# A list scheduler's durations, hops and holding times set to traced values, with new priorities for the prologue

## The chip, the cores and the metric

The kernel runs on one core of one Trainium2 chip. The metric is device time in microseconds (us) of one launch; the time before is the median of three runs. A core has five engines that run their own instruction streams and wait for each other by semaphores: PE (matmul; its weight loads are listed as PEld), DVE (vector), ACT (scalar), POOL (GpSimd) and SP, which here issues all DMAs.

## What is computed

Three stages follow each other. Linear attention over 4 batches, 8 heads, 576 positions and 64 columns gives x of 2304 x 512. A mixture of 8 experts with weights from a softmax and 8 rounds of row and column normalisation (Sinkhorn) follows, and then a gated feed-forward layer.

```python
def _attn_ref(q, k, v):
    q_s = exp(q - max(q, -1)); q_s = q_s / (sum(q_s, -1) + 1e-09)
    k_s = exp(k - max(k, 2));  k_s = k_s / (sum(k_s, 2) + 1e-09)
    kv = einsum('bhsd,bhse->bhde', k_s, v)
    return einsum('bhsd,bhde->bhse', q_s, kv)

def _moe_ref(x, w_gate, w1, w2):
    P = exp(x @ w_gate - max)
    for _ in range(8):
        P /= P.sum(1, keepdims=True) + 1e-09
        P /= P.sum(0, keepdims=True) + 1e-09
        P *= N / E
    return sum(P[:, e:e+1] * (maximum(x @ w1[e], 0) @ w2[e]) for e in range(E))

def _moe2_ref(x, w_in, w_out):
    h = x @ w_in
    return (h * clip(h + 3, 0, 6) / 6) @ w_out
```

## The kernel before

**Matmuls.** Operands are split into a high and a low float16 half, so a product takes three matmuls for each 128 rows of depth. On top of that, 2 x 2 block products are formed in Strassen's way with seven products: `forms` makes the seven combinations of x (QB11, QT1, QB21, QB22, QT2, QT3, QT4) and `w1_steps` those of a weight block. Both end in `split`: ACT writes the high half, DVE the low half. One product is six matmuls of 384 columns.

**Steps.** The work behind the attention is 20 weight steps s (16 for the experts, 4 for the last layer) by 3 pairs p of token groups. `up_burst` makes the hidden layer of one (s, p), its copies out of PSUM run on ACT (`ring_r<-b`), and `down_tile` multiplies it with the second weights and adds to `acc`. While one (s, p) runs on PE, the weights of step s + 1 are loaded, scaled and split.

**The prologue.** Attention is done for two pairs of batches; the first stands ahead of everything. Its steps, with the tiles that they write: `load_k`, `load_q`, `load_v` (SP); `kmax` (DVE, `scr`), `ktr` (PE transposes), `mT` (DVE reduce, `ring_c`), `kback` (PE), `ksub` (DVE, `xbuf<-xbuf,b`), `kexp` (ACT, `xbuf<-xbuf`); `vcopy` (two chunks on ACT, two on POOL, `xbuf<-acc`); `kv` (PE, 64x65 matmuls, one set for each of four chunks c), which needs `kexp(c)` and `vcopy(c)`; `kvout` and `kvmax` (DVE), which divide and take the largest entry, one PE matmul with `identb` to spread it, and `pow2`, which makes a power-of-two scale `sx`. For the queries: `qmax` (DVE, `ring_qm<-acc`), `qsub` (POOL, `acc`), `qexp` (ACT, `acc<-acc`), `qsum` (DVE), `qn_` (DVE and POOL, `ring_r<-acc,ring_qm`), `qtr` (PE transposes `units,ring_r` and an ACT copy `ring_h<-b`). `xset` multiplies the transposed queries with the scaled kv (`ring_h,xbuf`, 64x192) and opens `forms`. Beside this the first weight block goes through `a1scale` (four squares on ACT, `w1buf<-raw`, then the same matmul with `identb`), `a1sums` (POOL) and `a1` (splits); the second weights through `a2`. The marks with 0 and 1 ahead are the attention of the first and the second pair; `w11` and `w21` are the two weight blocks of the second weight step.

**What sets the order.** Nothing is issued as it is written. `Planner` records every instruction, gives each a duration (`cost`, line 177) and a latest start worked out backwards from its users (`order`, line 295), less an entry of the table `EARLIER` (line 41) for the step's mark: a larger number puts a step ahead. `lay` (line 317) then places instructions one by one, with the engines' free times, a lock that DVE and POOL share, and waits between engines from `hop` (line 286). The order of placement is the order of issue on each engine. Where the plan has a pause of over 400 ns on PE ahead of 130 us, `issue` (line 444) puts matmuls in whose result nobody reads (`warm`, line 2383, in the trace `b<-units,plus`, L2385); their number is worked out from the planned pause. All other instructions carry line 472, where the recorded calls are issued, so they are told apart by their tiles.

Of the kernel before, what the change touches and what calls it, by code (L numbers as in the profile page):

```python
# [40 lines left out]
EARLIER = {  # L41
    "0kback": -30000.0,
    "0kexp": -52000.0,
    "0kmax": -26500.0,
    "0ksub": 500.0,
    "0kv_": 1000.0,
    "0kvout": -1000.0,
    "0load_k": 7000.0,
    "0load_q": -500.0,
    "0qsub": 19000.0,  # L50
    "0qsum": -9500.0,
    "0vcopy": -4000.0,
    "1load_v": 2000.0,
    "1qmax": -500.0,
    "1qn_": -15000.0,
    "1qsum": -11000.0,
    "a1load": 3000.0,
    "a1scale": -3500.0,
    "a1sums": -73500.0,
    "conv": 0000.0,  # L60
    "max": 40000.0,
    "w11": 500.0,
}
# [10 lines left out]
class Planner:  # L74
# [6 lines left out]
    SLACK = 60000.0  # L81
    HOP = 120.0
    MARGIN = 300.0
    NEAR = 4000.0
    GIVE = 100.0
# [91 lines left out]
    def cost(self, eng, name, out, ins):  # L177
        n = 1
# [3 lines left out]
        if eng == "tensor":  # L182
            passes = 1.0
            if out.dtype == F32 and ins[0].dtype == F32:
                passes = 2.0 if name == "transpose" else 4.0 if ins[0].shape[0] > 64 else 1.5
            return 2.0 + n * 0.4167 * passes
        if eng == "scalar":
            return 170 + 0.8 * n if psum else (720 if n == 512 else 180 + 0.9 * n)
        big = max([n] + [self.width(x) for x in ins])
# [96 lines left out]
    def hop(self, a, b):  # L286
        if a["eng"] == b["eng"] and a["eng"] != "sync":
            return 0.0
        if a["eng"] == "tensor":
            return 170.0 + self.HOP  # L290
        if a["eng"] == "sync":
            return a.get("land", 2500.0 + a["dma"] / 150.0)
        return self.HOP + (self.MARGIN if b["eng"] == "tensor" else 0.0)

# [22 lines left out]
    def lay(self, ops, first):  # L317
# [7 lines left out]
        ahead = {e: [] for e in self.ENGINES}  # L325
        lag = shift = pipe = 0.0
        gone = set()
        for o in ops:
# [13 lines left out]
        def following(q, t, d):  # L342
# [5 lines left out]
            for o in reversed(q[-24:]):  # L348
# [8 lines left out]
                if u == v:  # L357
                    break
                u += o["dur"]
                v += o["dur"]  # L360
                k += 1
# [4 lines left out]
        def pick(e):  # L366
            f = free[e]
            c = []
            for o in waits[e]:
# [3 lines left out]
                if first and o["fill"] and e != "sync" and o["late"] + lag > s + self.NEAR:  # L373
                    room, fits = following(e, s, o["dur"])
                    if not fits:
                        s = max(s + 50.0, room + 1.0)
                    elif o["lock"]:
                        room, fits = following(other[e] + " lock", s, o["dur"])
                        if not fits:
                            s = max(s + 50.0, room + 1.0)  # L380
# [5 lines left out]
            if e not in ("tensor", "sync"):  # L386
                end = s + o["dur"]
                for x in sorted((x for x in c if x[0] < end and x[1] < d), key=lambda x: x[1]):
# [4 lines left out]
        while len(result) < len(ops):  # L393
# [18 lines left out]
            o["start"] = s  # L412
            end = s + o["dur"] * (1.0 if e == "tensor" else 1.05)
            if e == "sync":
                free[e] = s + 500.0
                pipe = max(pipe, s + 2000.0) + o["dma"] / 370.0
                o["land"] = pipe + 1500.0 - s
                end = s
            else:
                free[e] = end  # L420
            if o["lock"]:
                lock[e] = end
            if e in other:
# [1995 lines left out]
```

## Time and profile before

| | |
|---|---|
| runs | 1769.96, 1770.32, 1772.51 us, median 1770.32 us |
| span of the profiled execution (its own time by the profiler) | 1768.3 us |
| PE busy | 1750.0 us (99%) |
| DVE, ACT, POOL busy | 1411.4 (80%), 1251.0 (71%), 588.0 (33%) us |
| chain that ended last | PE 96%, DVE 2%, DMA 1% |

The profiled execution is one run under the profiler, and its span runs from the first to the last instruction. The median of the timed runs lies 2.0 us above that span. A PE that is busy 99% of the span can still be filled with matmuls that nobody needs; the chain lists them by their line.

### The profile page before, as it was taken

The numbers are of one execution on the slowest core, as the hardware profiler recorded it, in microseconds if no ns is written. First come the engines' busy times: TensorE is split into PE (matmuls) and PEld (weight loads), VectorE is DVE, ScalarE is ACT, GpSimd is POOL, SyncE is SP. The second block draws the span as 40 slices with busy tenths as digits, with TensorE's granted clock in tenths as the row PEclk, the third lists the DMA queues.
The fourth block names the chain that finished last, engine by engine and source line by source line (L and its number), as shares of the span: only waits on it lengthen the run. The fifth ranks groups of instructions, "written<-read, shape, count | busy, mean of one in ns | idle before, by whom it ended". The sixth has DMA issues, their size and how long they took to land.

```text
span 1768.3 us, 33908 instructions
## 1 busy us (share of the span) xinstructions
PE 1750.0 (99%) x13199; PEld 1218.1 (69%) x13199; DVE 1411.4 (80%) x2629; ACT 1251.0 (71%) x2807; POOL 588.0 (33%) x651
## 2 busy tenths in 40 slices
PE   7999999999999999999999999999999999999999
PEld 5555556777777777777777777777777555777776
DVE  7874877787888888888888888888888788777884
ACT  5856575667667686777778687768777677767673
POOL 3423343434444423232333322333323223223311
PEclk9999999999999999999999999999999999999999
DMA  9410322324242313020303122130312454402022
GB/s 293 121 69 1 117 84 74 99 98 154 98 161 96 111 37 105 25 87 25 119 21 119 37 93 63 49 105 25 105 49 93 87 100 136 150 25 87 1 87 84
DMA packets 103330, 154.25 MB, mean 87 GB/s; under 512 B 47744, under 2 KB 51840, under 8 KB 102912
## 3 DMA queue, kind: packets, MB, share of 16 engines
q1 hardware_dynamic: 103168, 152.08, 27.8%
q8 instruction: 103, 1.69, 0.4%
q14 instruction: 59, 0.48, 0.1%
HBM read 119.69 MB, written 24.12 MB: 81 GB/s over the span
## 4 chain that ended last, share of the span: by engine, by line
PE 96%; DVE 2%; issue 1%; DMA 1%; ACT 0%; POOL 0%; SPq 0%; DVEq 0%; POOLq 0%; ACTq 0%
PE b L472 95%; PE b L2385 1%; DMA xbuf<-in_k_dram 0%; DVE prob L472 0%; DVE acc L472 0%; DVE ring_r L472 0%; DVE xbuf L472 0%; DMA acc<-in_q_dram 0%; DVE ring_rs L472 0%; SPq L472 0%; ACT w2buf L472 0%; DVE scr L472 0%; DVE ring_cs L472 0%; POOL wtmp L472 0%; DVE ring_c L472 0%
## 5 line engine op out<-in xcount | busy, mean ns | idle before, releaser
L472 PE MATMUL b<-xbuf,w1buf 128*128 128x384 f16 x5040 | 910.6, 326 | 0.4 <-DVE ring_r L472 0.2
L472 PEld LDWEIGHTS <-w1buf 128*128 128x128 f16 x5040 | 491.5, 98 | 278.2 <-issue 1.8
L472 PE MATMUL b<-w2buf,ring_h 128*128 128x256 f16 (+2 forms) x3048 | 523.5, 308 | 0.0
L472 POOL TENSOR_TENSOR ring_h<-ring_r,ring_h 128x384 f16<-128x384 f32 x262 | 259.8, 993 | 693.4 <-ACT ring_h L472 632.7
L472 PEld LDWEIGHTS <-ring_h 128*128 128x128 f16 x3810 | 371.4, 98 | 155.9 <-issue 1.8
L472 ACT COPY b<-b 128x256 f32<-128x256 f32 (+1 forms) x686 | 253.8, 376 | 191.5 <-PE b L472 114.6
L472 DVE SCALAR_TENSOR_TENSOR acc<-b,ring_cf,acc 128x512 f32<-128x512 f32 x372 | 270.9, 746 | 120.7 <-PE b L472 94.3
L472 PEld LDWEIGHTS <-xbuf 128*128 128x128 f16 x3228 | 303.2, 98 | 75.5 <-DVE xbuf L472 1.1
L472 ACT ACTIVATE ring_r<-b 128x384 f32<-128x384 f32 x319 | 155.2, 488 | 94.9 <-PE b L472 87.7
L472 DVE SCALAR_TENSOR_TENSOR ring_r<-b,ring_r 128x384 f32<-128x384 f32 x215 | 118.7, 553 | 65.3 <-PE b L472 37.6
L472 PE MATMUL b<-xbuf 128*128 128x256 f16 (+1 forms) x1338 | 118.8, 251 | 2.2 <-issue 1.6
L472 POOL TENSOR_TENSOR raw<-raw 128x256 f32<-128x256 f32 (+1 forms) x119 | 102.0, 874 | 52.7 <-DVE w2buf L472 18.9
L472 POOL TENSOR_TENSOR ring_h<-scr,ring_h 128x384 f16<-128x384 f32 x40 | 38.8, 970 | 225.2 <-ACT ring_h L472 216.6
L472 ACT ACTIVATE ring_h<-ring_r 128x384 f16<-128x384 f32 x210 | 108.2, 521 | 7.7 <-DVE ring_r L472 5.4
L472 PE MATMUL b<-scr,xbuf 128*128 128x256 f16 x762 | 107.2, 273 | 0.1
L472 PE MATMUL b<-w2buf,xbuf 128*128 128x256 f16 x762 | 107.2, 273 | 0.0
L472 PE MATMUL b<-kvs,xbuf 128*128 128x256 f16 x762 | 107.2, 273 | 0.0
L472 PE MATMUL b<-xbuf,ring_h 128*128 128x256 f16 x468 | 91.2, 273 | 0.0
L472 DVE SCALAR_TENSOR_TENSOR acc<-b,ring_co,acc 128x512 f32<-128x512 f32 (+1 forms) x82 | 60.3, 741 | 27.5 <-PE b L472 25.7
L472 DVE TENSOR_TENSOR xbuf<-scr,xbuf 128x384 f16<-128x384 f32 x126 | 76.9, 635 | 6.5 <-ACT xbuf L472 6.3
L472 DVE SCALAR_TENSOR_TENSOR w1buf<-raw,ring_ws,w1buf 128x512 f16<-128x512 f32 x100 | 79.2, 825 | 3.1 <-ACT w1buf L472 2.7
L472 ACT ACTIVATE scr<-b 128x384 f32<-128x384 f32 x113 | 54.8, 488 | 37.2 <-PE b L472 36.6
(197 smaller groups left out, 2128.2 us busy)
## 6 DMA issues: line engine op xcount, KB each, us to landing
xbuf<-xkeep SPq DMA_DIRECT2D x119, 384.0 KB, 3.5
raw<-in_moe_w_dram SPq DMA_DIRECT2D x31, 1024.0 KB, 5.5
scr<-in_moe_w_in_dram SPq DMA_DIRECT2D x13, 512.0 KB, 3.7
scr<-in_moe_w_out_dram SPq DMA_DIRECT2D x12, 512.0 KB, 3.4
xkeep<-xbuf SPq DMA_DIRECT2D x2, 2688.0 KB, 9.0
xkeep<-xbuf SPq DMA_DIRECT2D x14, 384.0 KB, 8.4
out_dram<-acc SPq DMA_DIRECT2D x18, 256.0 KB, 2.0
raw<-win SPq DMA_DIRECT2D x4, 1024.0 KB, 5.4
```

The lines of the kernel that those rows point to most:

```text
L472: f(*a, **k)
L2385: real.tensor.matmul(banks[t][:, : 2 * P], plus, some, start=True, stop=True, skip_group_check=True)
```

## The change

Three things are changed, and no instruction of the computation is added or removed.

1. `cost`, `hop` and the rules of `lay` get other numbers: durations for narrow float32 matmuls, ACT and POOL; a hop for each receiving engine (45 to 120 ns where 120 stood for all); a holding time `held`, which is less than the duration by 80 ns on DVE and ACT and 40 ns on POOL, since the next instruction may start that much ahead, and times 1.01 where durations were taken times 1.05; and for DMAs a limit of 8 in flight and another bandwidth.
2. The table `EARLIER` gets 35 entries in place of 21, nearly all of them for steps of the prologue.
3. As a result, instructions stand in another order on every engine, over the whole program, and the number of filling matmuls goes from 131 to 92.

```diff
 EARLIER = {
-    "0kback": -30000.0,
-    "0kexp": -52000.0,
...
-    "w11": 500.0,
+    "w11": -18000.0,
+    "w21": 21000.0,
 }
...
-    HOP = 120.0
+    HOP = {"vector": 45.0, "scalar": 45.0, "gpsimd": 95.0, "tensor": 65.0, "sync": 120.0}
+    OVERLAP = {"vector": 80.0, "scalar": 80.0, "gpsimd": 40.0}
+    IN_FLIGHT = 8
     MARGIN = 300.0
+    SLOW = 1.01
...
-                passes = 2.0 if name == "transpose" else 4.0 if ins[0].shape[0] > 64 else 1.5
+                passes = 2.0 if name == "transpose" else 4.0 if ins[0].shape[0] > 64 else 0.78
+            elif ins[0].shape[0] <= 64:
+                passes = 0.3
...
-            return 170 + 0.8 * n if psum else (720 if n == 512 else 180 + 0.9 * n)
+            return (170 + 0.8 * n if psum else 180 + 0.88 * n) + 90 * (len(ins) - 1)
...
-            if big == 512 and len(out.shape) > 2:
-                return 1610
-            return 70 + (2.25 if len(ins) > 1 else 1.2) * big
+            return 320 + 1.6 * big if len(ins) > 1 else 220 + 0.88 * big
...
+    def held(self, o):
+        return max(o["dur"] - self.OVERLAP.get(o["eng"], 0.0), 40.0) * (1.0 if o["eng"] == "tensor" else self.SLOW)
...
-            end = s + o["dur"] * (1.0 if e == "tensor" else 1.05)
+            end = s + o["dur"]
             if e == "sync":
+                if len(landed) >= self.IN_FLIGHT:
+                    s = max(s, landed[-self.IN_FLIGHT])
                 free[e] = s + 500.0
-                pipe = max(pipe, s + 2000.0) + o["dma"] / 370.0
-                o["land"] = pipe + 1500.0 - s
+                pipe = max(pipe, s + 1900.0) + o["dma"] / (310.0 if s < 4500.0 else 385.0)
+                landed.append(pipe + 200.0)
+                o["land"] = landed[-1] - s
                 end = s
             else:
-                free[e] = end
+                free[e] = s + self.held(o)
```

**Place 1: DVE behind the last `kmax`.** In the order of before DVE takes two query maxima (`ring_qm<-acc`), then the three remaining `mT` (`ring_c`), and the third of the remaining `ksub` (`xbuf<-xbuf,b`) stands behind a `qsum`:

```order
L472 TENSOR_TENSOR scr<-scr,xbuf 128x256
L472 TENSOR_REDUCE ring_qm<-acc 128x8x3 x2
L472 TENSOR_REDUCE ring_c_103<-b_67 128x2
L472 TENSOR_REDUCE ring_c_103<-b_68 128x2 x2
L472 TENSOR_TENSOR xbuf<-xbuf,b_65 128x1152
L472 TENSOR_TENSOR xbuf<-xbuf,b_66 128x1152
L472 TENSOR_REDUCE ring_qm<-acc 128x8x3
L472 TENSOR_TENSOR xbuf<-xbuf,b_66 128x1152
```

The same place on DVE in the changed order:

```order
L496 TENSOR_TENSOR scr<-scr,xbuf 128x256
L496 TENSOR_REDUCE ring_c_103<-b_67 128x2
L496 TENSOR_REDUCE ring_c_103<-b_68 128x2 x2
L496 TENSOR_REDUCE ring_qm<-acc 128x8x3 x2
L496 TENSOR_TENSOR xbuf<-xbuf,b_66 128x1152
L496 TENSOR_TENSOR xbuf<-xbuf,b_65 128x1152
L496 TENSOR_TENSOR xbuf<-xbuf,b_66 128x1152
L496 TENSOR_REDUCE ring_qm<-acc 128x8x3
```

The three `mT` have moved ahead of the two query maxima, and the three `ksub` follow each other.

**Place 2: ACT between the first `kexp` and the query copies.** In the order of before, three of the four weight squares (`w1buf_79,ring_c_107`), a `vcopy` (`xbuf<-acc`), a `qexp` (`acc<-acc`) and the fourth square stand ahead of the second `kexp`, and the last two `kexp` come last:

```order
L472 ACTIVATE w1buf_79,ring_c_107<-raw 128x512 x3
L472 COPY xbuf<-acc 128x18x64
L472 ACTIVATE acc<-acc 128x8x192
L472 ACTIVATE w1buf_79,ring_c_107<-raw 128x512
L472 ACTIVATE xbuf<-xbuf 128x1152
L472 ACTIVATE acc<-acc 128x8x192
L472 COPY xbuf<-acc 128x18x64
L472 ACTIVATE xbuf<-xbuf 128x1152 x2
L472 COPY ring_h<-b_68 128x384
```

The same place on ACT in the changed order, up to the fourth square:

```order
L496 ACTIVATE w1buf_79,ring_c_107<-raw 128x512 x2
L496 COPY xbuf<-acc 128x18x64
L496 ACTIVATE acc<-acc 128x8x192
L496 ACTIVATE xbuf<-xbuf 128x1152
L496 ACTIVATE acc<-acc 128x8x192
L496 ACTIVATE xbuf<-xbuf 128x1152 x2
L496 COPY xbuf<-acc 128x18x64
L496 ACTIVATE w1buf_79,ring_c_107<-raw 128x512
L496 COPY ring_h<-b_67 128x384
L496 COPY ring_h<-b_68 128x384
L496 ACTIVATE w1buf_79,ring_c_107<-raw 128x512
```

Two squares and the second `vcopy` have moved behind the last `kexp`, and the fourth square stands among the query copies (`ring_h<-b`).

**Place 3: ACT in the first (s, p).** In the order of before the four squares of the second step's weights (`w1buf_80,ring_c_107`) stand between two copies of products (`ring_r<-b`):

```order
L472 CAST ring_h<-ring_r 128x384
L472 ACTIVATE ring_r<-b_64 128x384
L472 ACTIVATE w1buf_80,ring_c_107<-raw 128x512 x4
L472 ACTIVATE ring_r<-b_61 128x384
L472 ACTIVATE ring_r<-b_64 128x384
```

The same place on ACT in the changed order, where the first square of `w1buf_80` comes after the first splits of the second weights (`w2buf_81<-acc`):

```order
L496 CAST ring_h<-ring_r 128x384
L496 ACTIVATE ring_r<-b_64 128x384
L496 ACTIVATE ring_h<-ring_r 128x384
L496 ACTIVATE ring_r<-b_64 128x384
L496 CAST ring_h<-ring_r 128x384
L496 ACTIVATE ring_r<-b_61 128x384
L496 ACTIVATE w2buf_81<-acc,ring_ws 128x512 x2
L496 ACTIVATE ring_r<-ring_r 128x384
L496 ACTIVATE ring_r<-b_61 128x384
L496 CAST ring_h<-ring_r 128x384
L496 ACTIVATE ring_r<-ring_r 128x384
L496 ACTIVATE w1buf_80,ring_c_107<-raw 128x512
```

The squares are now single and spread out, and two copies of `b_61` have moved ahead of them. On PE the first six half tiles of `down_tile` (`w2buf_81,ring_h`) stand accordingly ahead of the first product with `w1buf_80`, where before five products with `w1buf_80` stood ahead of any of them. On DVE the `qmax` of the second pair now stands ahead of the splits of `w1buf_80`, and before behind them.

## Rows read from the trace of the kernel before

**Rows 1.** The page: span, and busy time of PE and its weight loads.

```profile
span 1768.3 us, 33908 instructions
PE 1750.0 (99%) x13199; PEld 1218.1 (69%) x13199; DVE 1411.4 (80%) x2629; ACT 1251.0 (71%) x2807; POOL 588.0 (33%) x651
```

**Rows 2.** Windows: stretch, length, busy us by engine (instructions), PE clock, DMA share, GB/s.

```profile
300.00:400.00 100.00, 100.00 (x734) 71.56 (x733) 78.47 (x141) 66.74 (x153) 35.39 (x42) 1.00 0.30 97
```

**Rows 3.** Timeline of PE: start us, us, what [idle before <-releaser].

```profile
13.76 2.02 PE L2385 MATMUL b<-units,plus 128*128 128x256 f16 x17
18.39 1.10 PE L472 MATMUL b<-units,ring_c 128*64 128x128 f32 x8 [2.61 <-DVE ring_c L472]
...
24.95 1.28 PE L472 MATMUL b<-xbuf 64*64 64x65 f32 x72
...
27.46 0.35 PE L472 MATMUL b<-xbuf 64*64 64x65 f32 x8
...
35.32 0.22 PE L472 MATMUL b<-identb,ring_c 128*128 128x128 bf16 x1
...
37.17 2.22 PE L472 MATMUL b<-ring_h,xbuf 64*64 64x192 f32 x48 [0.43 <-DVE xbuf L472]
...
61.46 6.01 PE L472 MATMUL b<-xbuf,w1buf 128*128 128x384 f16 x36
```

**Rows 4.** Timeline of DVE, 13 to 37 us.

```profile
13.01 0.42 DVE L472 TENSOR_TENSOR scr<-scr,xbuf 128x256 f32<-128x256 f32 x1
14.72 3.42 DVE L472 TENSOR_REDUCE ring_qm<-acc 128x24 f32<-128x1536 f32 x2 [1.29 <-DMA acc<-in_q_dram]
18.05 0.68 DVE L472 TENSOR_REDUCE ring_c<-b 128x2 f32<-128x128 f32 x3
19.10 2.62 DVE L472 TENSOR_TENSOR xbuf<-xbuf,b 128x1152 f32<-128x1152 f32 x2 [0.37 <-PE b L472]
...
23.67 1.34 DVE L472 TENSOR_TENSOR xbuf<-xbuf,b 128x1152 f32<-128x1152 f32 x1
...
33.22 0.23 DVE L472 TENSOR_SCALAR ring_c<-b 128x4 f32<-128x4 f32 x2 [3.74 <-PE b L472]
...
36.76 0.35 DVE L472 TENSOR_SCALAR xbuf<-xbuf,sx 128x256 f32<-128x256 f32 x1
```

**Rows 5.** Timeline of ACT, 18 to 53 us.

```profile
18.82 0.63 ACT L472 ACTIVATE w1buf<-raw 128x512 f16<-128x512 f32 x1
...
20.49 1.48 ACT L472 ACTIVATE acc<-acc 128x1536 f32<-128x1536 f32 x1
...
24.93 1.14 ACT L472 COPY xbuf<-acc 128x1152 f32<-128x1152 f32 x1
25.97 2.21 ACT L472 ACTIVATE xbuf<-xbuf 128x1152 f32<-128x1152 f32 x2
28.32 0.48 ACT L472 COPY ring_h<-b 128x384 f32<-128x384 f32 x1
...
34.79 0.48 ACT L472 COPY ring_h<-b 128x384 f32<-128x384 f32 x1 [0.20 <-PE b L472]
...
52.50 0.62 ACT L472 ACTIVATE w1buf<-raw 128x512 f16<-128x512 f32 x1
```

**Rows 6.** Timeline of POOL, around 17 us.

```profile
16.56 5.51 POOL L472 TENSOR_TENSOR acc<-acc,ring_qm 128x1536 f32<-128x1536 f32 x2 [15.20 <-DVE ring_qm L472]
```

**Rows 7.** The chain that ended last, 40 to 62 us: start us, us, what.

```profile
41.08 1.64 PE b L2385 x14
...
61.18 0.44 PE b L2385 x4
```

**Rows 8.** Waits of PE over the span: us in total, times, longest us.

```profile
PE b L472 <- DVE ring_cs L472: 0.8, 2, 0.5
...
PE b L472 <- DVE ring_r L472: 0.2, 1, 0.2
```

**Rows 9.** Windows of 1 us in the prologue; the columns are those of rows 2.

```profile
19.00:20.00 1.00, 1.00 (x9) 0.52 (x6) 0.90 (x1) 1.00 (x3) 1.00 (x2) 0.50 1.05 389
```

More of the change, by code (lines that the diff above doesn't have):

```diff
@@ L41 @@
 EARLIER = {
-    "0kback": -30000.0,
-    "0kexp": -52000.0,
-    "0kmax": -26500.0,
     "0ksub": 500.0,
-    "0kv_": 1000.0,
+    "0ktr": 1500.0,
+    "0kv_": 17000.0,
     "0kvout": -1000.0,
-    "0load_k": 7000.0,
+    "0load_k": 7500.0,
     "0load_q": -500.0,
+    "0load_qlast": 13000.0,
+    "0load_v": -7000.0,
     "0qsub": 19000.0,
     "0qsum": -9500.0,
-    "0vcopy": -4000.0,
-    "1load_v": 2000.0,
+    "0qtr": 14000.0,
+    "0vcopy": -5000.0,
+    "1kback": 3500.0,
+    "1kexp": 1500.0,
+    "1kmax": -1000.0,
+    "1ksub": -1500.0,
+    "1ktr": 14000.0,
+    "1kv_": 6000.0,
+    "1kvout": -500.0,
+    "1load_k": 2500.0,
+    "1load_v": 2500.0,
     "1qmax": -500.0,
-    "1qn_": -15000.0,
-    "1qsum": -11000.0,
+    "1qn_": 7000.0,
+    "1qsub": -3500.0,
+    "1qsum": -11500.0,
+    "1qtr": 26500.0,
     "a1load": 3000.0,
-    "a1scale": -3500.0,
+    "a1scale": -16500.0,
     "a1sums": -73500.0,
-    "conv": 0000.0,
-    "max": 40000.0,
-    "w11": 500.0,
+    "a2": -1000.0,
+    "forms": 28000.0,
+    "max": 41500.0,
+    "second": 8500.0,
+    "w11": -18000.0,
+    "w21": 21000.0,
 }
@@ L326, in lay @@
         lag = shift = pipe = 0.0
+        landed = []
         gone = set()
@@ L358, in following @@
                     break
-                u += o["dur"]
-                v += o["dur"]
+                u += self.held(o)
+                v += self.held(o)
                 k += 1
@@ L373, in pick @@
                 if first and o["fill"] and e != "sync" and o["late"] + lag > s + self.NEAR:
-                    room, fits = following(e, s, o["dur"])
+                    room, fits = following(e, s, self.held(o))
                     if not fits:
@@ L377, in pick @@
                     elif o["lock"]:
-                        room, fits = following(other[e] + " lock", s, o["dur"])
+                        room, fits = following(other[e] + " lock", s, self.held(o))
                         if not fits:
@@ L386, in pick @@
             if e not in ("tensor", "sync"):
-                end = s + o["dur"]
+                end = s + self.held(o)
                 for x in sorted((x for x in c if x[0] < end and x[1] < d), key=lambda x: x[1]):
@@ L412, in lay @@
             o["start"] = s
-            end = s + o["dur"] * (1.0 if e == "tensor" else 1.05)
+            end = s + o["dur"]
             if e == "sync":
+                if len(landed) >= self.IN_FLIGHT:
+                    s = max(s, landed[-self.IN_FLIGHT])
                 free[e] = s + 500.0
-                pipe = max(pipe, s + 2000.0) + o["dma"] / 370.0
-                o["land"] = pipe + 1500.0 - s
+                pipe = max(pipe, s + 1900.0) + o["dma"] / (310.0 if s < 4500.0 else 385.0)
+                landed.append(pipe + 200.0)
+                o["land"] = landed[-1] - s
                 end = s
             else:
-                free[e] = end
+                free[e] = s + self.held(o)
             if o["lock"]:
-                lock[e] = end
+                lock[e] = free[e]
             if e in other:
```

4 lines of the change are left out of this document (2 added, 2 removed).

## Prediction

> **What bounds the kernel now.** I read the page first: PE is busy for 1750.0 of 1768.3 us [rows 1]. Then the windows of 100 us: from 300 us on PE is busy in every one, with DVE at 78% and ACT at 67% beside it [rows 2]. The work of PE is the same before and after, so only what PE loses can be won: idle time, and the filling matmuls (L2385), which look busy. The timeline of PE and the chain show where that is. PE's first lasting work stands behind the spread of the largest kv entry at 35.32 us and the first `xset` at 37.17 us [rows 3]; from there the chain lists eight blocks of filling matmuls with 39 in all, the largest 1.64 us for 14, the last 0.44 us for 4 [rows 7]; from 61.46 us products follow each other at 6.01 us for 36, 0.163 us each [rows 3]. Later PE waits 0.8 us in two places for the Sinkhorn sums and hardly elsewhere [rows 8]. So there are three things to win: the start of `xset` (call it X), the fillings between X and 61.46 us, and the Sinkhorn waits.
>
> **X, the keys on DVE (place 1).** `kmax` ends at 13.43 us, and DVE idles 1.29 us for the queries until 14.72; the three `mT` come at 18.05 and take 0.68 us [rows 4]. In the new order they stand ahead of the maxima. The transposes they need are issued ahead of the fillings of 13.76 us [rows 3], so they run from about 14.1 to 14.8, in the idle time, and cost the queries 0.1 us. The maxima take 3.42 us, to 18.2; then three `ksub` of 1.34 us follow without the `qsum` between them, to 22.2 us, where the third ended at 25.0 [rows 4].
>
> **X, the keys on ACT (place 2).** Before, the last two `kexp` end at 28.18 us [rows 5]. Now two squares (0.63 us and a read of the sum, 0.75 each) and a `vcopy` (1.14) are no longer ahead of them. What they wait for instead is the second `qexp`, whose `qsub` on POOL ends at 16.56 + 5.51 + 0.1 = 22.2 us [rows 6]: 22.2 + 1.5 for `qexp` + 2.2 for two `kexp` = 25.9 us, and the moved `vcopy` ends at 27.0. `kv` of the last chunk needs both, so from 27.1 us; it takes 1.28 us alone [rows 3], and about 0.5 us for each of two groups of query transposes between, with 0.2 us of waits: it ends near 29.5 us. Before, DVE waited for it until 33.22 us [rows 4]. From there to the matmul that spreads the largest entry took 35.32 - 33.22 = 2.1 us, so by this path it could come at 31.7 us.
>
> **X, the second release.** At 35.32 us this matmul was released by two things at once: its bank is that of the last query transposes, whose copy on ACT ends at 34.79 + 0.48 = 35.27 us [rows 3, 5]. There are eight copies, the first at 28.32. In the new order the first can start at 27.0 + 0.75 (one square) = 27.75 us, two copies take 0.8 us, then comes the fourth square (0.75), and six copies remain. With kv out of PE's way each bank goes copy 0.48, transposes 0.35, two handovers of 0.1 to 0.2: 1.15 us a bank, two banks, so 0.57 us a copy. 29.3 + 6 x 0.57 = 32.7 us. This is later than 31.7 and decides. The bounds: 31.7 (copies fully hidden), and 27.75 + 0.75 + the old 6.95 us for eight copies = 35.4 (no gain). I take 32.7, since what spread the old eight copies over 6.95 us was PE, which ran the kv of two chunks between them from 27.46 us [rows 3], and one of these now runs ahead of them. From there to X took 37.17 - 35.32 = 1.85 us; the small DVE operations that the new order puts into it (a copy to `mx`, a second column each of `ws` and `sx`) are of the kind that follow each other in 0.06 to 0.15 us: +0.1. X moves from 37.17 to 34.65: **-2.5 us**, between -3.6 and 0.
>
> **From X to steady products (place 3).** 39 filling matmuls stood here; the new program has 19, in three blocks, all ahead of the fourth product. At 0.11 us each [rows 7] that is 4.3 against 2.1 us. What lets them go: at 52.50 us ACT started four squares of `w1buf_80`, 3.0 us in all [rows 5], ahead of a copy of `b_61` that PE needed for its next product; four of the eight blocks (15 matmuls) come around or behind them. Now the copies stand first, and half tiles of `down_tile` fill PE while the second half's copies run. Walking the new order from X with the durations of the old rows, I find three waits without fillings, some 1.1 us in all, since ACT is nearly full there: two of them in front of products that continue in one bank and need the copy of their last state, one for QT3's copies. So the loss goes from 4.4 to 3.2 us: **-1.2 us**, between -2.3 and 0.
>
> **Behind that.** DVE's `qmax` of the second pair now stands ahead of the `w1buf_80` splits. Its queries are loaded into columns that the second weights occupy until their last split, so if the load is late, the splits queue behind the waiting `qmax`, and PE, which comes to the first `w1buf_80` product a few us later, behind them. No row shows this; the nearest is DVE's wait for the first queries, 1.29 us [rows 4]. Bounds 0 and +1.3; I take **+0.2**, since six half tiles and two products stand on PE between the last `w2buf_81` split and that product. In the Sinkhorn part the two waits of 0.8 us [rows 8] come where 6 products' and 12 half tiles' matmuls (384 columns at 0.163 us [rows 3], 512 at a third more, 3.6 us) stand between two column sums, or even less; in the new order one such gap is left and the others hold 4.3 to 7.5 us of matmuls: **-0.8 us**, between -0.8 and 0. For the steady part, with the engines beside PE at 67 to 78% [rows 2], I take 0: a shorter planned holding time moves work by tenths of a microsecond there, and PE's operands lie ready for longer. That cover is the point on which the slower case turns.
>
> **Sum.** -2.5 - 1.2 + 0.2 - 0.8 = -4.3 us on a span of 1768.3. The median is 2.0 us above the span; taking the difference over to it, 1770.32 - 4.3 = 1766.0 us.
>
> [...]
>
> **Rivals.** (1) X comes earlier, but little is won behind it, or X is held by the query copies to half: -1.0 to -3.3 us, near 1768 us. For it: ACT and DVE are nearly full between X and 61 us, so that what is taken from one place stands in another. Against it: the squares are 3.0 us of ACT work that is plainly in the wrong place. The low clock at X ends here too, with 0.04 of its chance. (2) Nothing moves: the copies and the bank bind as before, X stays, and the fillings are only replaced by bare waits: 1769.5 to 1770.3. Against it: the order of ACT ahead of the last `kexp` is shorter by 2.6 us whatever the plan believes. (3) Slower, by the steady part: there are 54 turns (18 weight steps by three pairs) behind the prologue. With shorter holding times the plan has less in hand, and fill work (the splits of the next weights) may slip ahead of a copy that PE waits for. The one such wait in the rows is 0.2 us [rows 8]; once in each turn it is 10.8 us, so 1776.8 us. It decides from 0.08 us a turn on (4.3 / 54), and from 0.15 us the kernel is slower by over 0.2%. For it: the order changes throughout, and before nothing was lost here, so it can only get worse. Against it: 22% of DVE and 33% of ACT are free [rows 2].
>
> **How the numbers follow.** About 0.2%, 3.5 us, is what a measurement of this kernel can tell from no change. The forecast (-3.5 to -6.4 us, 1763.9 to 1766.8): 0.58. Rival 1: 0.26, rival 2: 0.06, rival 3 at its smaller sizes (within 0.2% in the end): 0.03, at its larger: 0.07. So faster 0.58, the same 0.35, slower 0.07. The range leaves out the best tail and most of the slower case: 1763.8 to 1769.8 us.
>
> **What would show it.** Right: the `identb` matmul at 32.7 us and X near 34.7; `ring_h<-b` copies 0.57 us apart; 19 filling matmuls behind X and continuous products from about 54 us; PE waits for `ring_cs` under 0.3 us. Wrong: the last copy near 35 us (X not moved); new idle PE between 50 and 70 us behind `qmax`; PE busy under 99.9% in the windows behind 300 us, which alone would make it slower.

## The result and the profile after

The changed kernel takes 1783.86 us (median of four runs, 1781.53 to 1786.79) where the kernel before takes 1770.14 (median of four runs, one more than in its table): a ratio of 1.0077, with a 95% interval of 1.0063 to 1.0092. It is slower by some 14 us; 1766.0 had been predicted. The profiled execution took 1781.53 us with a span of 1779.7.

The page of the changed kernel, span and PE, answers to [rows 1]; below it, from the same page, the shares of the chain that ended last:

```profile
span 1779.7 us, 33849 instructions
PE 1752.8 (98%) x13160; PEld 1216.9 (68%) x13160; DVE 1382.2 (78%) x2629; ACT 1244.3 (70%) x2807; POOL 580.7 (33%) x651
...
PE 86%; DVE 5%; DMA 5%; ACT 3%; issue 1%; SPq 0%; POOL 0%; DVEq 0%; ACTq 0%
```

PE's share of the chain fell from 96% to 86%, and DMA's rose from 1% to 5%. Windows of 100 us of the changed kernel, with the columns of [rows 2], show that PE no longer fills the steady part:

```profile
300.00:400.00 100.00, 99.69 (x726) 70.76 (x725) 83.00 (x149) 68.26 (x156) 39.03 (x45) 1.00 0.34 115
...
1000.00:1100.00 100.00, 99.05 (x760) 74.08 (x759) 79.48 (x152) 74.01 (x174) 27.96 (x32) 1.00 0.19 61
1400.00:1500.00 100.00, 98.00 (x527) 51.20 (x526) 84.46 (x166) 73.67 (x143) 28.44 (x28) 1.00 0.59 125
```

To place the loss, I take from each trace the time from one matmul's start to the next one's, less the median of that step for the same shape in the kernel before, and add up what is over; of a filling matmul the whole step counts. This gives PE's lost time by stretch, in us, beside the start of the first `xset` (X). Each row is one profiled execution, so that differences of a microsecond ahead of 130 us can be the execution's own: `changed` and e3 have the same order up to there.

| kernel | X | 0-60 | 60-130 | 130-250 | from 250 |
|---|---|---|---|---|---|
| before | 37.17 | 32.6 | 11.0 | 4.8 | 5.8 |
| changed | 36.96 | 31.1 | 16.3 | 5.2 | 13.6 |
| e1 old landing | 43.76 | 36.2 | 14.0 | 5.2 | 6.2 |
| e2 before, new landing | 38.01 | 35.4 | 10.0 | 3.5 | 17.1 |
| e3 half loads | 34.55 | 28.6 | 15.3 | 5.2 | 5.6 |
| e4 fillings moved | 38.73 | 32.8 | 16.5 | 5.2 | 19.4 |
| e5 new landing early only | 35.31 | 29.4 | 14.8 | 6.1 | 6.7 |
| e6 priorities only | 35.67 | 31.9 | 15.2 | 5.4 | 6.2 |
| e7 durations only | 40.73 | 34.6 | 13.1 | 5.0 | 7.5 |
| e8 loads held | 35.15 | 30.3 | 12.5 | 6.5 | 6.5 |
| e9 old plan behind | 37.27 | 32.6 | 13.3 | 5.0 | 6.2 |
| e10 old plan from X | 35.38 | 29.1 | 14.8 | 4.6 | 6.0 |
| e11 before, longer landing | 36.91 | 33.6 | 11.2 | 3.8 | 5.4 |
| e12 first pair only | 34.93 | 30.6 | 12.5 | 4.4 | 5.9 |
| e13 old second pair | 35.13 | 30.2 | 12.4 | 6.8 | 7.5 |
| e14 = e12, longer landing | 35.18 | 31.4 | 11.9 | 3.8 | 5.7 |
| e15 = e12 again | 34.75 | 30.5 | 12.3 | 4.4 | 5.8 |

Changed against before: -1.5 ahead of 60 us, +5.3 up to 130, +0.4 up to 250, +7.8 behind: 12.0 us, against 11.4 us between the spans.

**What a loss in the steady part looks like.** The chain of the changed kernel from 1029 to 1041 us (start us, us, what), for one wait of PE. PE idles nine times for over 0.3 us behind 250 us, and in eight of them the steps that lead up to the wait begin with a weight load, as here:

```profile
1029.87 6.31 DMA raw<-in_moe_w_dram
...
1036.20 0.73 ACT w1buf L496 x2
...
1036.96 0.72 ACT w1buf L496 x2
1037.68 0.38 ACT ring_r L496
...
1038.11 2.93 PE b L496 x21
```

A load of weights lands 6.31 us after its issue. ACT stands idle for 1.64 us at the first square of that block (`w1buf<-raw`), up to 1036.20, and the copy `ring_r<-b`, which needs none of this data, stands behind two squares in ACT's order and comes at 1037.68. PE waits for that copy. So a late load reaches PE through a copy that does not use it. Waits of ACT over the whole span (us in all, times, longest us), those on weight loads, of the kernel before:

```profile
ACT w1buf L472 <- DMA raw<-in_moe_w_dram: 7.3, 4, 5.5
...
ACT w2buf L472 <- DMA raw<-wout: 2.4, 1, 2.4
ACT w2buf L472 <- DMA raw<-in_moe_w_dram: 2.1, 2, 1.4
```

and of the changed kernel:

```profile
ACT w2buf L496 <- DMA raw<-in_moe_w_dram: 12.2, 6, 3.6
...
ACT w1buf L496 <- DMA raw<-in_moe_w_dram: 11.9, 8, 6.5
...
ACT w2buf L496 <- DMA raw<-wout: 4.8, 4, 2.0
```

11.8 us in 7 waits became 28.9 us in 18. The change, called "another bandwidth" where it was described, plans a 1 MB load to land 1.9 + 1048576 / 385000 + 0.2 = 4.8 us after its issue, where 2.0 + 2.8 + 1.5 = 6.3 us stood before; 1.4 of the 1.5 us between them are the fixed part, not the bandwidth. What they take was there to read in the trace of before, in its list of DMA issues (KB each, median us from issue to landing):

```profile
raw<-in_moe_w_dram SPq DMA_DIRECT2D x31, 1024.0 KB, 5.5
raw<-win SPq DMA_DIRECT2D x4, 1024.0 KB, 5.4
raw<-wout SPq DMA_DIRECT2D x4, 1024.0 KB, 6.2
```

In the changed kernel they take the same: 5.3, 5.3 and 6.4 us. Half of them are later than the change plans by half a microsecond or more, and none of the 39 lands in less than 4.88 us (4.86 in the kernel before).

**The prologue after.** PE's timeline of the changed kernel, 14 to 39 us, against [rows 3]:

```profile
14.79 2.03 PE L2409 MATMUL b<-units,plus 128*128 128x256 f16 x17
19.24 0.44 PE L496 MATMUL b<-units,ring_c 128*64 128x128 f32 x4 [2.42 <-DVE xbuf L496]
20.91 2.23 PE L496 MATMUL b<-xbuf 64*64 64x65 f32 x72 [1.23 <-ACT xbuf L496]
23.07 2.74 PE L2409 MATMUL b<-units,plus 128*128 128x256 f16 x12
25.74 1.73 PE L496 MATMUL b<-xbuf 64*64 64x65 f32 x72
...
36.96 2.18 PE L496 MATMUL b<-ring_h,xbuf 64*64 64x192 f32 x48 [0.34 <-DVE xbuf L496]
```

and one of six windows of 1 us from 20 to 26 us, the granted clock third from the end:

```profile
23.00:24.00 1.00, 1.00 (x13) 0.68 (x6) 1.00 (x1) 1.00 (x2) 1.00 (x1) 0.50 0.06 15
```

PE idles 2.42 and 1.23 us behind the fillings, and the granted clock stands at 0.50 from 20.0 to 26.8 us. The first `kv` set takes 2.23 us, where 72 such matmuls took 1.28 in the kernel before at a granted clock of 1.00 [rows 3], and then the plan's 12 fillings stand ahead of the second set: 2.74 us. The second set starts at 25.74, although its `kexp` on ACT ended at 23.30. ACT itself starts its first weight square when the first weight load lands, and then works without a pause to the last `kexp`:

```profile
18.14 0.63 ACT L496 ACTIVATE w1buf<-raw 128x512 f16<-128x512 f32 x1 [6.49 <-DMA raw<-in_moe_w_dram]
...
24.57 2.20 ACT L496 ACTIVATE xbuf<-xbuf 128x1152 f32<-128x1152 f32 x2
```

### The profile page after: what moved, and what is told of

Read it like the earlier page. It is cut to its first block, busy times and chain, and to the rows that moved or that the text cites. A ratio compares the mean times of both kernels' runs of the same rounds, so it can differ in the third digit from the quotient of the medians.

```text
span 1779.7 us, 33849 instructions
## 1 busy us (share of the span) xinstructions
PE 1752.8 (98%) x13160; PEld 1216.9 (68%) x13160; DVE 1382.2 (78%) x2629; ACT 1244.3 (70%) x2807; POOL 580.7 (33%) x651
## 3 DMA queue, kind: packets, MB, share of 16 engines
q8 instruction: 103, 1.69, 0.4%
## 4 chain that ended last, share of the span: by engine, by line
PE 86%; DVE 5%; DMA 5%; ACT 3%; issue 1%; SPq 0%; POOL 0%; DVEq 0%; ACTq 0%
PE b L496 85%; DMA raw<-in_moe_w_dram 2%; DVE w1buf L496 2%; DVE scr L496 1%; DMA raw<-wout 1%; ACT w2buf L496 1%; ACT w1buf L496 1%; DVE ring_r L496 1%; DMA acc<-in_v_dram 0%; DVE acc L496 0%; ACT ring_r L496 0%; DMA xbuf<-scr 0%; DMA acc<-in_q_dram 0%; DVE xbuf L496 0%; ACT ring_h L496 0%
## 5 line engine op out<-in xcount | busy, mean ns | idle before, releaser
L496 POOL TENSOR_TENSOR raw<-raw 128x256 f32<-128x256 f32 (+1 forms) x119 | 94.5, 818 | 20.4 <-issue 17.0
L496 ACT CAST ring_h<-ring_r 128x384 f16<-128x384 f32 x133 | 67.0, 508 | 21.4 <-DVE ring_r L496 20.6
L496 DVE TENSOR_TENSOR xbuf<-scr,xbuf 128x384 f16<-128x384 f32 x126 | 72.3, 584 | 11.5 <-ACT xbuf L496 11.3
L496 ACT CAST xbuf<-scr 128x384 f16<-128x384 f32 x132 | 66.3, 507 | 16.5 <-DVE scr L496 15.9
```

What stands on the lines that cost most here:

```text
L496: f(*a, **k)
```

## Experiments

Two theories for the steady part stood at the start. **A**: the new landing figures put ACT's squares where their weights are not there yet. **B**: the shorter holding times and hops do it (the third rival of the prediction). **C** was for the prologue: the low clock, 0.50, and the fillings at that clock hold the second `kv` set. All ratios are against the kernel before on the same chip.

**e1: the landing figures undone in the changed kernel.**

```diff
-                if len(landed) >= self.IN_FLIGHT:
-                    s = max(s, landed[-self.IN_FLIGHT])
                 free[e] = s + 500.0
-                pipe = max(pipe, s + 1900.0) + o["dma"] / (310.0 if s < 4500.0 else 385.0)
-                landed.append(pipe + 200.0)
-                o["land"] = landed[-1] - s
+                pipe = max(pipe, s + 2000.0) + o["dma"] / 370.0
+                o["land"] = pipe + 1500.0 - s
```

> The changed kernel with one thing undone: the plan again takes the kernel before's figures for the landing of a load (about 6.3 us for 1 MB, where the change says about 4.8), without the limit of 8 in flight. The new durations, hops, holding times and priorities stay. Theory A (the steady part loses because ACT's squares stand where their weights have not landed, and the copies that PE needs queue behind them): the losses of the steady part, some 8 us behind 100 us, vanish, and the time falls from 1783.9 to 1770 to 1775 us; ACT's waits on raw fall from 29 us in all to under 12. Theory B (shorter holding times and hops cost the steady part, the third rival of the prediction): the waits stay, 1778 to 1785 us. By both the prologue stays as in the changed kernel.

Measured: 1776.47 us, ratio 1.0031 (1.0021 to 1.0041). The steady part is whole again (6.2 us behind 250 us), and ACT's waits on weight loads are 11.6 us (6.9, 2.7 and 2.0). The time missed the expected 1775 because the prologue did not stay as it was: X came at 43.76, 6.6 us later than before, as much as the whole difference in time. A stall of 2.36 us, shown with e4 and e8, is part of it, and behind the stall the clock stands at 0.50 from 32.0 to 38.8 us.

**e2: the new landing figures alone, in the kernel before.** The diff of e1 backwards.

> The kernel before with one thing of the change: the new figures for the landing of a load and the limit of 8 in flight. Durations, hops, holding times and priorities are the old ones. Theory A: the squares move ahead of their data here too; slower than before by 3 to 10 us, 1773 to 1780 us, with PE waiting behind ACT in the steady part. Theory B: 1769 to 1772 us.

Measured: 1782.15 us, ratio 1.0065 (1.0050 to 1.0080), 2 us above the range expected by A. A few lines on loads make the old plan 12 us slower with no other number touched: 11.3 us more are lost behind 250 us. A is confirmed from the other side. The limit of 8 in flight, which e1 and e2 switch together with the figures, cannot be the cause: behind 55 us of either plan it holds no load back. One of its longest waits, in the chain (start us, us, what):

```profile
1276.99 7.64 DMA raw<-in_moe_w_dram
...
1284.66 0.73 ACT w1buf L477 x2
...
1286.14 0.28 ACT b L477
...
1286.46 1.63 PE b L477 x13
```

**e3: the changed kernel's order, with half the bytes in each later weight load.**

```diff
...
+        if eng == "sync" and name == "dma_start" and out.tensor.name.startswith("raw") and self.halve:
+            call = (call[0], (), dict(out=k["out"][:, :2], in_=k["in_"][:, :2]))
...
```

> The changed kernel's order of instructions, unchanged, but from the second weight step on each weight load brings only the first two of four row chunks (0.5 MB in place of 1 MB); the other half of the tile keeps older weights, so the matmuls are as many but not the reference's. A load then lands some 1.3 to 2 us sooner. Theory A: the waits of PE in the steady part shrink, 1774 to 1779 us. Theory B: the order is at fault, not the data's landing, and the time stays within 1782 to 1785 us.

Measured: 1772.11 us, ratio 1.0003 (0.9993 to 1.0012), 12 us less than the changed kernel with every instruction in its place. Loss behind 250 us: 5.6. The issues of this run, in the columns as above:

```profile
raw<-in_moe_w_dram SPq DMA_DIRECT2D x29, 512.0 KB, 3.9
...
raw<-win SPq DMA_DIRECT2D x4, 512.0 KB, 3.8
raw<-wout SPq DMA_DIRECT2D x4, 512.0 KB, 4.1
```

Now most of the loads land ahead of the planned 4.8 us, and most of the waits are gone. The gain is larger than the 5 to 10 us expected, partly because the prologue was better in this execution (X at 34.55, in the same program up to there): the first weight load landed 1.3 us sooner. ACT's first square of e3, against 18.14 above:

```profile
16.80 0.63 ACT L499 ACTIVATE w1buf<-raw 128x512 f16<-128x512 f32 x1 [5.46 <-DMA raw<-in_moe_w_dram]
```

**e4: 38 fillings ahead of the first `kv` set in place of 17, and 2 behind it in place of 12.**

```diff
-                        warm(best, int((pause - 150) * self.FILLED[o["start"] > self.COLD] / 109))
+                        count = int((pause - 150) * self.FILLED[o["start"] > self.COLD] / 109)
+                        warm(best, self.FILL_AT.get(blocks, count))
+                        blocks += 1
...
+    FILL_AT = {4: 38, 5: 2}
```

> The changed kernel with two blocks of filling matmuls in the prologue changed in number: the block ahead of the first kv from 17 to 38, the block between the first and the second kv from 12 to 2; nothing else moves. Theory C (idle PE ahead of the first kv lets the granted clock fall to 0.50, and 12 fillings at that clock then hold the second kv): the clock stays at 1.00 to the first kv, the second kv starts near 23.5 us in place of 25.74, the first xset at 34.5 to 35.5 us in place of 36.96, and the time falls by 1.5 to 2.5 us against the changed kernel, to 1781.4 to 1782.4 us. Otherwise (ACT's copies of the queries hold it in any case): the second kv comes earlier, the first xset stays at 36.5 to 37 us and the time at 1783 to 1785 us.

Measured: 1788.40 us, ratio 1.0102 (1.0087 to 1.0117), above both expected ranges. C was right on the clock and on the second set, which starts at 23.06 us with the clock at 1.00 up to there and beyond. But X came later, at 38.73. PE's timeline of e4, in the fourth set:

```profile
27.70 0.85 PE L500 MATMUL b<-xbuf 64*64 64x65 f32 x41
31.18 0.34 PE L500 MATMUL b<-xbuf 64*64 64x65 f32 x7 [2.63 <-issue]
```

PE stands for 2.63 us in the middle of a group, waiting for nothing that the profile shows (`issue`). The DMA queues of e4 (packets, MB, share of 16 engines) from 24 to 28.8 us:

```profile
q1 hardware_dynamic: 2231, 1.24, 101.4%
```

and from 28.8 to 30:

```profile
q1 hardware_dynamic: 344, 0.39, 94.3%
q8 instruction: 1, 0.02, 4.6%
```

The profile calls the queue q8 `instruction`. It moves packets of 16 KB: 103 of them over the span for 13171 matmuls and as many weight loads, one for 128 matmuls (1.69 MB in 103 packets in the kernel before). I read them as PE's instructions because the counts fit; the profile does not name the engine. In e4 the second packet behind 20 us starts at 28.89 us, after PE has stopped, with the loads of the second pair's values (256-byte pieces) and keys (2304-byte pieces) filling the DMA engines from 24 us on. e1 stops behind the same matmul of the program, the 349th, for 2.36 us, and its packet comes at 30.30. PE goes on 1.4 us after the packet's end in both. In the kernel before the packet came at 27.42 and the 349th matmul at 31.6. So the new theory: **D**, the next block of PE's instructions queues behind those loads. Most of the rest of e4's time was lost behind 250 us (19.4 against 13.6 us in the same order). Why is not shown: all four runs of e4 are slower than the slowest of the changed kernel. On the time itself e4 says little.

**e5: the new landing figures only for loads planned ahead of 30 us**, the old ones behind.

```diff
+    EARLY = 30000.0
...
+                if s < self.EARLY:
...
+                else:
+                    pipe = max(pipe, s + 2000.0) + o["dma"] / 370.0
+                    o["land"] = pipe + 1500.0 - s
```

> The changed kernel, but the new figures for the landing of a load hold only for loads planned ahead of 30 us; from there on the plan uses the kernel before's figures. PE's order is that of the changed kernel to beyond the first xset, filling matmuls included. Theory A (landing figures cost the steady part): PE's idle time behind 250 us falls from about 8 us to about 3 us (to what the kernel with the old landing figures throughout showed), the first xset stays at 34.5 to 37 us, and since the prologue of this one is 5 us or more better than with the old landing figures throughout (first xset there at 43.8 us), the time is 1768 to 1773 us. Theory B (shorter holding times): 1778 us or more.

Measured: 1773.01 us, ratio 1.0013 (1.0003 to 1.0022), at the upper end of the expected range. With PE's order unchanged through the prologue, the time falls by 11 us; 6.7 us are lost behind 250 us.

**e6 and e7: one half of the rest alone.** e6 is the kernel before with the new `EARLIER` table; e7 is the changed kernel with the old table and the old landing figures.

```diff
 EARLIER = {
-    "0kback": -30000.0,
-    "0kexp": -52000.0,
+    "0ktr": 1500.0,
+    "0kv_": 17000.0,
...
```

> The kernel before with only the new priorities; durations, hops, holding times and landing are the old ones. Theory A: the steady part is that of before, and what is lost is lost in the prologue, since the priorities were set for other numbers: 1769 to 1775 us. Theory B has nothing to lose here either: the same. If the priorities themselves cost the steady part: over 1777 us.

> The changed kernel with the old priorities and the old landing figures: only durations, hops and holding times are new. Theory A: PE idles less than 2 us behind 250 us, and the time is within 1768 to 1776 us, by what the prologue makes of it. Theory B: the steady part loses 5 us or more, 1776 to 1784 us.

Measured: e6 1775.37 us (1.0029; 1.0017 to 1.0041), e7 1777.24 us (1.0037; 1.0024 to 1.0050), both above their expected ranges, e6 by 0.4 us. Neither loses much in the steady part (6.2 and 7.5 against 5.8 us). e6 has X 1.5 us earlier and loses 4 us between 60 and 130 us. e7 has X at 40.73: its plan puts 30 fillings behind the first `kv` set, and at a granted clock of 0.50, which lasts to 25.7 us, they take 4.90 us and hold the second set until 27.55. Either alone costs 5 to 7 us, in the prologue and the second pair. Both together, with the old landing figures, cost as much (e1, 6.5 us), and 2.8 us with the new figures ahead of 30 us (e5).

**e8: e5, the fillings of e4, and the second pair's key and value loads planned from 40 us on.** On SP they then stand behind the load of the second weights.

```diff
+                if o["mark"] in ("1load_k", "1load_v"):
+                    s = max(s, self.HOLD)
...
+    HOLD = 40000.0
```

> The kernel with the new landing figures ahead of 30 us only, and two things more: the two blocks of filling matmuls ahead of and behind the first kv are 38 and 2 in place of 17 and 12 (as in the run that stalled for 2.6 us), and the loads of the second pair's keys and values are planned from 40 us on, so that they stand behind the load of the second weights on SP. If the stall in the third and fourth kv set came from PE's next 16 KB of instructions waiting behind those loads on the DMA engines: no idle PE without a releaser in the kv sets, the packet of the instruction queue within 1.5 us of the 220th matmul, and the first xset at 34 to 35 us, 1767 to 1771 us. If it came from the kv sets being closer together: the same stall of 2 to 3 us at the 348th matmul, the first xset near 38 us, 1770 to 1775 us.

Measured: 1772.75 us, ratio 1.0011 (1.0002 to 1.0021), somewhat above the expected range; but of the stall 0.27 us are left. The same place on PE in e8:

```profile
27.71 0.85 PE L509 MATMUL b<-xbuf 64*64 64x65 f32 x41
28.83 0.34 PE L509 MATMUL b<-xbuf 64*64 64x65 f32 x7 [0.27 <-issue]
...
35.15 2.18 PE L509 MATMUL b<-ring_h,xbuf 64*64 64x192 f32 x48 [0.34 <-DVE xbuf L509]
```

and its DMA queues from 24 to 28 us, with nothing but the instructions:

```profile
q8 instruction: 1, 0.02, 2.2%
```

The `kv` sets are as close together as in e4, so it was the loads, and D holds: the six later kernels with these loads held have the packet 1.6 to 2.4 us behind the 220th matmul, where it took 4.9 us in e4 and 5.7 in e1. Which loads the packet queues behind is not shown: in e5 they fill the DMA engines from 25 to 27 us as well, and the packet comes 0.9 us behind the 220th. In e8 the packet, at 25.86, comes 1.8 us behind that matmul (24.02), not within the 1.5 us expected. X at 35.15, just above the expected 34 to 35, is within 0.5 us of the 34.65 that the prediction had wanted. That the time is still not below the kernel before shows that X is not what the time follows: 1.5 us more than before are lost between 60 and 130 us and 1.7 between 130 and 250.

**e9, e10: the old durations, hops and holding times from some point on**, as e8 otherwise: from 130 us of the plan's PE time (e9), from 15 us (e10).

```diff
...
-        dur = self.cost(eng, name, out, ins)
+        dur = (self.cost if self.clock < self.CUT else self.cost_old)(eng, name, out, ins)
...
```

> The kernel with the loads held and the fillings moved, and besides, from 130 us of the plan's PE time on, the durations, hops and holding times of the kernel before. This leaves the new numbers to the prologue and the two first weight steps. If the new holding times cost the steady part a rest of some 3 us (the waits at 1433 us and 1555 us behind DVE's fill work, which all three kernels with new holding times and old landing figures show and the kernel before does not): these go, the span behind 250 us is that of before, and the time falls from 1772.8 to 1769 to 1771 us. If they belong to something else: 1772 to 1774 us.

> The same, but with the old durations, hops and holding times from 15 us of the plan's PE time on, that is from about the first products on. Up to the first xset it is the new order with loads held: first xset near 35.2 us, 2 us ahead of before. If what is won there is kept: 1767.5 to 1769.5 us. If it is given back between 50 and 250 us, as the other kernels with the new priorities did: 1770 to 1773 us.

Measured: e9 1769.96 us (0.9995; 0.9986 to 1.0004), e10 1771.59 us (1.0000; 0.9991 to 1.0008). e9's time is in the range of B's small share, but its profile places the gain only in part. The profiled execution took 1772.72 us, 2.8 above the median and the slowest of eleven, and with the same plan as e8 up to 130 us it has X at 37.27, with the clock at 0.50 from 24.4 to 31.3 us. The waits behind DVE's work, seen in e8's chain near 1555 us, are gone:

```profile
1553.53 0.75 DVE acc L509
1554.28 0.47 DVE ring_r L509
1554.75 0.47 DVE xbuf L509
1555.22 0.67 DVE acc L509
...
1555.91 0.37 ACT b L509
...
1556.32 2.78 PE b L509 x24
```

(two fills, `ring_r` and `xbuf`, stand ahead of the `acc` that frees the bank). Smaller ones came in their place: behind 250 us e9 loses 6.2 where e8 loses 6.5. Of the 1.8 us that e9 loses less behind 130 us, 1.5 are ahead of 250 us, not where the expectation had looked. e10 gives back what it wins at X, as its second expectation said: 14.8 us are lost between 60 and 130.

**e11: the kernel before with a landing 1.0 us later (7.3 us for 1 MB).**

```diff
-                o["land"] = pipe + 1500.0 - s
+                o["land"] = pipe + (1500.0 if s < 30000.0 else 2500.0) - s
```

> The kernel before with a landing planned 1.0 us later than its own figure, for loads from 30 us on (7.3 us for 1 MB). If the old figure of 6.3 us already covers what loads take (5.1 to 6.7 us), more changes nothing that can be told: 1768.5 to 1771.5 us, with PE's idle time behind 250 us as before. If the steady part follows the figure in both directions: 1 us or more faster than before, under 1769 us.

Measured: 1770.65 us, ratio 0.9997 (0.9988 to 1.0006): no difference. In this order the figure costs only on one side: 1.5 us less than the old one is 12 us, 1.0 us more is nothing. The range of 5.1 to 6.7 us in the expectation is too narrow: behind 100 us, 35 of the 36 such loads of the kernel before took 4.86 to 7.37 us, 6 of them more than the planned 6.3, and one took 12.45.

**e12, e13: old priorities for the steps of the second pair and of the second weight step**, e12 on e10 and e13 on e8.

> As the kernel with the old plan from 15 us on, but with the new priorities only for the steps of the first pair and the first weights; those of the second pair and of the second weight step are the old ones. If the new priorities of the second pair's steps cost time between 50 and 130 us: 1767 to 1769 us, below the kernel before. If not: within 1 us of the kernel with all new priorities and the old plan from 15 us on.

> The kernel with the loads held, the fillings moved and the new landing figures ahead of 30 us only (1772.75 us), with one thing more undone: the steps of the second pair and of the second weight step have their old priorities. New durations, hops and holding times hold throughout. If these priorities cost time between 60 and 130 us (as 1771.6 against 1769.6 us suggests where the old plan stands behind them): 1769.5 to 1771.5 us. If not: 1772 to 1774 us.

Measured: e12 1769.58 us (0.9991; 0.9982 to 1.0000), between its two expected ranges and 2.0 us under e10, and its loss between 60 and 130 us falls from 14.8 to 12.5. e13 1773.48 us (1.0012; 1.0003 to 1.0021), with 12.4 us there against 12.5 in e8: nothing. So these priorities cost 2 us under the old durations and nothing under the new ones. As the cause of the loss between 60 and 130 us under the new durations the theory fell.

**e14, e15: e12 with the longer landing, and e12 once more.** e14 is e12 with the 2500.0 of e11 in place of 1500.0.

> The kernel with the new plan for the first pair only (1769.6 us), and a landing planned 1.0 us later (7.3 us for 1 MB) from 30 us on. If a reserve above the measured 5.1 to 6.7 us is worth something: 1768 to 1769 us. If it is covered already: 1769 to 1770.5 us.

> The kernel with the new plan for the first pair only, once more, to tell whether it is faster than the kernel before: 0.1% faster if the 2 us that its first xset comes earlier are kept, no difference if they are given back.

Measured: e14 1767.94 us, ratio 0.9983 (0.9974 to 0.9991); e15 1770.38 us (0.9996; 0.9987 to 1.0005). e14 beats both kernels, by 1.9 us against before, and its slowest of eleven runs (1768.64) is below the fastest of e15 (1769.01): in this order the longer landing is worth some 2 us. The two profiled executions do not show where: e14's took longer than its median and e15's is the fastest of its runs, so that their spans are 1766.6 and 1767.2 us, and e14's largest differences by stretch are +0.9 and -0.6 us. e12 and e15, one kernel on two chips, cannot be told from before.

## Why the prediction was wrong

**X, -2.5 us: reached in other executions of the same order, not in the profiled one.** X came at 36.96, not 34.65; in e3 and e5, whose order is the same up to there, it came at 34.55 and 35.31. The forecast has two legs. The first is the end of the last `kexp`: 26.77 (25.9 forecast). The prediction had it wait for `qsub` on POOL. In the runs ACT works from its first weight square to the end of the last `kexp` in 8.63 to 8.65 us in all eleven kernels with this order of ACT (the changed one, e3 to e5, e8 to e10, e12 to e15), so what sets it is the landing of the first weight load: a square at 18.14 us here, at 16.80 in e3, at 17.58 in e5. That 25.9 lies amid the ends that came (25.4 to 26.8) is luck. The second leg, from there to X, took 10.2 us (8.8 forecast). Its forecast takes a `kv` set at the 1.28 us of before, at a granted clock of 1.00 [rows 3], and has no step for the 12 fillings that the plan puts between the first two sets. Here they ran at a granted clock of 0.50 from 23.07 to 25.8, and the second set waited for PE, not for ACT. In e3 and e5 it did so too, by 1.8 and 1.5 us, but there the clock was back at 1.00 from 23.4 and 23.2 us on, and the leg took 9.1 us. So of the 2.3 us that X is late, 0.9 is the load, some 1.1 goes with the longer stretch at the low clock, and 0.3 is the rest. The low clock was there to read in the trace of before, 0.50 behind 2.61 us of idle PE [rows 3, 9]. What sets it is not shown: here it is 0.50 from 20.0 to 26.8 us behind 2.42 us of idle PE, and 1.00 in the same windows of e4 and e8, where fillings covered the pause; but e10 and e14, with the same fillings, have 0.50 from 23 to 26.4 us. The low clock at X itself, to which rival 1 gives 0.04, is in no profile shown here: at X the granted clock is 1.00 in the changed kernel, in e5 and in e8, and the 48 passes of `xset` took 2.18 us in each. Moved fillings and held loads bring the leg to 8.9 to 9.4 us (e8, e10, e12 to e15), no better than e3 and e5.

**X to steady products, -1.2 us: about right.** Ahead of 60 us the changed kernel loses 1.5 us less than before with X nearly where it was, so the gain is between X and 60 us. It was given back at once.

**`qmax` and the second pair, +0.2: 5.3 us.** The bound taken, 1.3 us, looked at one queue. DVE did wait for those queries, 1.21 us at 66.86, and its queue ends PE's largest wait of this stretch, 1.15 us at 81.62 for a `ring_r`. The chain of the changed kernel between 72 and 90 us shows another queue:

```profile
74.51 4.94 DVE w1buf L496 x2
...
79.47 5.08 DMA raw<-in_moe_w_dram
...
84.57 0.73 ACT w2buf L496 x2
...
86.83 0.72 ACT w2buf L496 x2
87.56 1.06 ACT xbuf L496
...
88.66 1.66 PE b L496 x36
```

The load of the second step's second weights is late, four squares, 3.0 us of ACT, stand behind it, and then a `kexp` of the second pair, for which PE waits 0.63 us. The rest of the 5.3 us is spread over smaller waits. The old landing figures take 1.5 us off this stretch (e5), holding the loads together with the fillings another 2.3 (e8). These are differences of single executions. The last 1.5 us over the kernel before stay open; the new priorities of the second pair were tried (e13) and are not it.

**Sinkhorn, -0.8 us: right and outweighed.** From 200 to 250 us the same sum gives 0.70 us against 1.47. But from 130 to 200 us some 1.2 us more are lost, which the prediction had not looked at.

**Steady part, 0: the term that decides, and the step that failed.** It is +7.8 us. The prediction asked here only what holding times and hops do, and found 22% and 33% of DVE and ACT free as cover [rows 2]. It passed over the third group of numbers in the same diff, the landing of loads, whose durations the trace of before would have given: 1 MB loads there take 5.4 to 6.2 us in the median, where the change plans 4.8. Undoing these figures alone, or halving the loads in the same order, takes the loss back to 6.2 and 5.6 us (e1, e3), against 5.8 before. That ACT is idle a third of the time is no cover when it stands at an instruction whose data is late (28.9 us in 18 waits) and the copy that PE needs comes behind that instruction. The third rival had the right place and size, 54 turns and 1776.8 us, with the wrong mechanism (fills that slip ahead, by shorter holding times), and was given 0.10. Its own mechanism is worth at most 0.4 to 1.7 us behind 250 us, by the kernels with new holding times and old landing figures there (e1, e5, e7, e8, e13). What it named as the sign to look for, PE under 99.9% in the windows behind 300 us, is what came.

**The range** ended at 1769.8 because no part of it bounded the landing from both sides.

## To carry to other kernels

In a list scheduler a planned landing time is a promise on behalf of an engine that, like ACT at 1036 us, takes up nothing of what stands behind a waiting instruction: plan a load above what most of the trace's loads take, not at its best or its middle, since a figure that is too short stalls everything queued behind the consumer. Here 4.8 us, less than any of 39 loads took, cost 12 us; 6.3, longer than 30 of the 39, did not; and 7.3 cost nothing, and in another order even won some 2 us. Durations, priorities and landing figures set one order together: the new priorities of the second pair cost 2 us under the old durations and nothing under the new ones, and durations or priorities alone cost 5 to 7 us. So a change of several is measured as a whole and each part alone. When a stage is to start earlier, look at what else must come earlier with it: the load that its first engine waits for, the clock (here 0.50 for 6.8 us), the filling work that was sized for another pause, and the instructions themselves.

## What was not expected of the hardware

As I read the traces, PE ran out of instructions. In bursts of 64x65 matmuls, 72 in 1.28 us [rows 3], 128 of them, one packet of 16 KB of the instruction queue by the count in e4, take about 2.3 us, an estimate from these two numbers, and where the loads of the second pair's keys and values fill the DMA engines, the next packet can come late: 2.36 us of stall in e1 and 2.63 in e4 at the same matmul of the program, 0.27 in e8 with these loads out of the way. In the second pair's burst the kernel before has it too, 1.6 us behind 92 us; its packet ends at 92.4, and PE goes on 1.4 us after that, as in e1 and e4.

The same program's first weight load let ACT start its squares at 16.80 us in one execution and at 18.14 in another, and X moved by 2.4 us (e3 and the changed kernel, alike up to there): 1.3 us by the load, the rest with a clock that stood at 0.50 up to 23.4 us in the one and up to 26.8 in the other. A gain of 2 us in such a prologue needs many runs to be seen at all.
